# Talking-heads attention and a gated layer on one core: the first evictions, the second batch's scores and the order around the maximum

## The chip, the core and the metric

The kernel runs on one core of a Trainium2 chip. The core has TensorE (PE) for matrix products, VectorE (DVE), ScalarE (ACT) and GpSimd (POOL) for work on elements, and SyncE (SP), whose queue issues nearly all DMA transfers here. Each engine works through its own instructions in order; semaphores tie them together. The metric is the device time of one execution in microseconds (us).

## The reference

Attention with two mixings of the heads, and then a feed-forward layer with a gate. Cut to what matters:

```python
# q, k, v: (4, 12, 448, 64); w_pre, w_post: (12, 12)
scores = scale * np.matmul(q, k.transpose(0, 1, 3, 2))
scores = np.einsum('bhij,hg->bgij', scores, w_pre)
scores = scores - np.max(scores, axis=-1, keepdims=True)
attn = np.exp(scores)
attn = attn / (np.sum(attn, axis=-1, keepdims=True) + 1e-09)
attn = np.einsum('bhij,hg->bgij', attn, w_post)
x = np.matmul(attn, v)               # then to (4*448, 768)
h = x @ w_in                         # w_in: (768, 2048), float64 in memory
g = h * (1.0 / (1.0 + np.exp(-1.702 * h)))
out = g @ w_out                      # w_out: (2048, 768), float64 in memory
```

## The kernel before

**Steps.** The unit of the attention is a group of 10 query rows times 12 heads, which fills 120 partitions. A batch has 45 such groups, so there are 180 steps, and one loop over the step number `i` writes the whole program down. Of step `i` it issues, in this order: the gather of group `i + 4` out of a scratch tensor in DRAM (`gather`, SP's queue), the product that mixes the heads of group `i + 1` (`mix`, two instructions on PE), the second mixing of group `i - 2` (`post_whole`, PE, batch 0), the copies of its result for group `i - 3` (`keep_whole`, batch 0), the weights of the second mixing of group `i - 1` (`weigh_mix`, POOL), the maximum of group `i` (`peak`, L286, DVE), its exponential with the sum (`expo`, L293, ACT; the sum gets its small term on POOL, L299), then the jobs that are due (`run_jobs`), pieces of the feed-forward layer, score products, products with v, and last the reciprocal (`inverse`, L304, DVE). The next step's maximum stands behind that reciprocal on DVE.

**Scores.** They are made ahead, for a chunk of up to 120 query rows and one pair of heads at a time: `scores` (PE) into two banks of PSUM, `keep_scores` (copies to a tile `sc`, of which there are three), `send_scores` (SP's queue, to the scratch tensor `sd`). Batch 0 multiplies q and k in float32 (L233). Batches 1 to 3 split each operand into an upper and a lower float16 part and add three products (L243). For that, k and q of a batch are loaded once for a sum of squares (`squares`, ACT, six instructions of half a third each), a product with ones that adds it over the partitions (`join`, PE, then DVE), and small instructions on DVE for the scale (`scale`); and loaded again to be split (`upper_part` on ACT or POOL, `lower_part`, L201, on DVE). Batch 1's pairs are due in steps 34 to 73.

**Copies of mixed weights.** In batch 0, `post_whole` leaves 48 columns of blocks in one bank `pp` of PSUM; `keep_whole` copies it in two halves, the first on ACT (L385), the second on DVE (L382) or on ACT, by a count of what each engine has been given. Both stand ahead of the step's maximum and exponential. The two engines read one bank, so the second copy waits for the first.

**Jobs and tokens.** Each step gives every engine a budget of 4.3 (estimated us), kept up to 4.5. A job has a first step, what it must follow, an engine and an estimated cost; it is issued when its engine has half its cost left, or at once where it is marked urgent. The conversions of w_in and w_out are such jobs: 16 pieces, one due every five steps from step -6 on, each of three fetched parts (three buffers `w64`), five DVE instructions a part that turn float64 into float32 (L495 to L515), squares on ACT, a scale, an upper part and a lower part (L548, DVE), and a store.

**Start.** q and k of batch 0 come in thirds on SP's queue; then DVE builds the matrices of both mixings (`mixing`, `mixing_pair`, the latter with `wall`), and the first chunk's six pairs are made, evicted (one head on ACT, one on DVE), and sent, with the jobs of steps -6 to -1 between them. The first gathers stand behind the last send.

The order on every engine is thus fixed when the program is written; nothing is chosen on the chip.

Of the kernel before, what the change touches and what calls it, by code (L numbers as in the profile page):

```python
# [38 lines left out]
def attention_then_feed_forward(ctx, tc, q, k, v, w_pre, w_post, w_in, w_out, out):  # L39
# [81 lines left out]

    def load_whole(name, i):

        t = st[name, 0, i] = flow.tile(SH[name], F32, name=f"{name}f{i}_0", tag=f"{name}p{i}")
        w = t.shape[1]
        nc.sync.dma_start(out=t, in_=SRC[name][0][:, i * w:(i + 1) * w])

# [35 lines left out]
    def mixing(b):  # L163
        wa = keep.tile([KG, KG], F32, name=f"wa_{b}", tag="wa", bufs=2)
        if b == 0:
            nc.vector.tensor_scalar_mul(wa, w_mix.rearrange("p i g -> p (i g)"), 0.125)
            st["wa", b] = wa
            return
# [54 lines left out]
    def scores(b, c, pr, tag=("gen", 3)):  # L223
# [4 lines left out]
        w = NPAIR // THIRDS  # L228
        if b == 0:
            qf, kf = st["q", 0, pr // w], st["k", 0, pr // w]  # L230
            for x in range(2):
                rs = slice(x * D, (x + 1) * D)
                nc.tensor.matmul(  # L233
                    two[x][:n, :S], qf[rs, pr % w, i0:i0 + n], kf[rs, pr % w, :],
                    start=True, stop=True,
                )
            return two, done
# [131 lines left out]

    def keep_whole(i):  # L370
        b, g = steps[i]
        n = rows_of(g)[1]
        c, off = g // GPC, (g % GPC) * GI
        pp = row.pop(("pp", i))
        w = NR // 2
        for x in range(2):
            if off == 0:
                st["p", b, c, x] = mixed.tile([CP, w, H, CI], F32, name=f"pf{x}_{b}_{c}", tag=f"p{x + 1}")
            o = st["p", b, c, x].rearrange("p r h i -> p (r h) i")[:, :, off:off + n]
            src = pp[:, x * w * H:(x + 1) * w * H, :]  # L380
            if x and tokens["D"] > tokens["A"]:
                nc.vector.tensor_copy(o, src)  # L382
# [360 lines left out]
    for b in range(1, B):  # L743
        z = GPB * b
        sizes = {}
        for name, first, ready in (("k", z - 25, z - 17), ("q", z - 23, z - 17), ("v", z - 8, z + LAG + 7)):
            sq = []
            for i in range(THIRDS):
                a = staged(first, [], name, b, i, "a")
                sq.append(job(0, {"A": 1.6}, 0, lambda eng, name=name, i=i, b=b: squares(name, b, i, eng, 2),  # L750
                              after=[(a, SENT)], urgent=True))
# [3 lines left out]
            for i in range(THIRDS):  # L755
# [4 lines left out]
                a["stage"][1].extend([up, lo])  # L760
        job(0, "D", 0.4, lambda b=b: mixing(b), after=[sizes["k"], sizes["q"]], urgent=True)

# [61 lines left out]
    for i in range(THIRDS):  # L824
        for name in "kq":
            load_whole(name, i)
    for i, w in enumerate((w_pre, w_post)):
        nc.scalar.dma_start(out=wrep[:, i, :], in_=w.unsqueeze(0).to_broadcast([GI, H, H]))
    nc.scalar.dma_start(out=wall, in_=w_post.unsqueeze(0).to_broadcast([128, H, H]))
    nc.vector.memset(ones, 1.0)  # L830
    last_pp.append(ps.tile([128, 512], F32, name="sums", tag="av", bufs=1))
    nc.vector.memset(tops, 0.0)
    nc.scalar.activation(warm, tops[:, 0:1], AF.Exp)
# [14 lines left out]
    )  # L848
    mixing(0)
    def mixing_pair():  # L850
# [21 lines left out]

    mixing_pair()
    tags = [("gen", 3), ("mx", 2), ("pp", 2)]
    for pr in range(NPAIR):
        two, done = scores(0, 0, pr, tags[pr % 3])
        for x in done:
            x["done"] = True
        t = keep_scores(0, 0, pr, two, "AD")
        refill(2.0)  # L880
        run_jobs(pr - NPAIR)
        send_scores(0, 0, pr, t)
    for i in range(AHEAD):
        gather(i)
    for i in range(THIRDS):
        load_whole("v", i)
    sq = [job(1, {"A": 1.6}, 0, lambda eng, i=i: squares("v", 0, i, eng, 2), urgent=True) for i in range(THIRDS)]
    j = job(1, "D", 0.2, lambda: join("v", 0), after=sq, urgent=True)
# [52 lines left out]
    while quanta or i < N + LAG + 12:  # L941
# [12 lines left out]
        if 0 <= i - 3 < GPB:  # L954
            keep_whole(i - 3)
        if GPB <= i - LAG - 1 < N:
# [12 lines left out]
        if i < N:  # L969
            peak(i)  # L970
            spend("D", 0.62)
            expo(i)
            spend("A", 0.82)
        run_jobs(i)
        slot()
# [83 lines left out]
```

## Time and profile before

| | us |
|---|---|
| median of 3 runs | 1081.61 (1077.75 to 1081.65) |
| the profiled execution, in all | 1085.16 |
| its span, from the first instruction to the last | 1083.4 |
| PE busy | 934.9 |
| DVE busy | 656.2 |
| ACT busy | 595.4 |
| POOL busy | 383.5 |
| mean clock of PE, as a share of full speed | 0.935 |

The profile is one execution. An engine's busy time says how full it was on the whole; where a stage has its limit is read from the stretches and from what each engine waited for. A wait is put down to whatever came last by the profile. In the timeline an instruction of the second kind, "SPq", is an issue of a DMA by SP's queue. A count such as x3 stands for instructions merged in one row.

### The profile page before, as it was taken

How to read it: one execution, taken by the hardware profiler on the slowest of the kernel's cores; microseconds unless marked ns; L12 is line 12 of the kernel's file. 1: busy time of each engine (PE TensorE's matmuls, PEld its weight loads, DVE VectorE, ACT ScalarE, POOL GpSimd, SP SyncE). 2: the span in 40 equal slices, each digit the busy share in tenths (PEclk: the TensorE clock that was granted, in tenths of full speed). 3: DMA queues.
4: the chain of work that ended last, by engine and by line, in shares of the span. 5: the costliest groups of instructions: out<-in, count | busy, mean ns of one | idle time of the engine just before them, and what ended most of it. 6: DMA issues, size and time to landing. Idle time of an engine off the chain costs nothing.

```text
span 1083.4 us, 20018 instructions
## 1 busy us (share of the span) xinstructions
PE 934.9 (86%) x7344; PEld 549.3 (51%) x7344; DVE 656.2 (61%) x1444; ACT 595.4 (55%) x1389; POOL 383.5 (35%) x567
## 2 busy tenths in 40 slices
PE   3576766686779788889989899999899999999998
PEld 1244544463445454455546455556555666555554
DVE  4477856779878779655554457455654566433334
ACT  2455564656756766655655766665656555323332
POOL 0122212225534246443443255334534444200221
PEclk7689978988699998999999899999999999999999
DMA  7778777776757754755557456745564432234332
GB/s 247 229 270 313 258 259 229 246 243 213 246 162 247 226 196 145 248 168 154 150 186 224 148 174 193 224 141 162 181 205 142 142 107 82 88 114 142 117 117 80
DMA packets 67430, 200.95 MB, mean 185 GB/s; under 512 B 7764, under 2 KB 32468, under 8 KB 67332
## 3 DMA queue, kind: packets, MB, share of 16 engines
q1 hardware_dynamic: 66928, 199.59, 57.5%
q8 instruction: 58, 0.95, 0.4%
q14 instruction: 40, 0.33, 0.1%
q10 hardware_dynamic: 404, 0.09, 0.1%
HBM read 143.02 MB, written 56.62 MB: 184 GB/s over the span
## 4 chain that ended last, share of the span: by engine, by line
PE 59%; DVE 21%; ACT 8%; DMA 7%; issue 4%; SPq 0%; POOL 0%; ACTq 0%; DVEq 0%; POOLq 0%
PE po L637 18%; PE h L598 17%; PE mx L279 8%; PE av L420 4%; PE qk L243 3%; DVE nm L286 3%; DVE w_p L548 2%; PE pp L356 2%; DMA r<-sd 2%; DMA sd<-sc 2%; PE pp L358 2%; PE pp L357 2%; ACT waste L96 2%; DVE w_f L509 2%; DVE w_f L515 2%
## 5 line engine op out<-in xcount | busy, mean ns | idle before, releaser
L637 PE MATMUL po<-g,wt 128*128 128x448 f16 x1152 | 248.2, 359 | 10.7 <-DVE th L619 6.2
L598 PE MATMUL h<-x,wt 128*128 128x448 f16 x1152 | 244.1, 355 | 4.4 <-ACT sc L253 2.5
L279 PE MATMUL mx<-r,wa 120*120 120x448 f32 x360 | 187.7, 605 | 60.6 <-ACT e L293 38.6
L343 POOL TENSOR_TENSOR a<-w,a 120x448 f16<-120x448 f32 x135 | 150.8, 1117 | 124.3 <-issue 69.4
L637 PEld LDWEIGHTS <-wt 128*128 128x128 f16 x1152 | 110.5, 99 | 133.3 <-issue 49.6
L329 POOL TENSOR_SCALAR w<-e,rs 120x448 f32<-120x448 f32 x135 | 91.0, 674 | 239.6 <-DVE rs L304 220.4
L598 PEld LDWEIGHTS <-wt 128*128 128x128 f16 x1152 | 109.2, 99 | 115.6 <-issue 29.7
L293 ACT ACTIVATE e<-mx,nm 120x448 f32<-120x448 f32 x180 | 113.3, 629 | 84.2 <-DVE nm L286 51.1
L337 ACT ACTIVATE a<-e,rs 120x448 f16<-120x448 f32 x135 | 91.0, 674 | 118.7 <-DVE rs L304 118.7
L667 DVE SCALAR_TENSOR_TENSOR acc<-po,ct,acc 128x448 f32<-128x448 f32 x141 | 96.0, 682 | 83.8 <-PE po L637 81.8
L616 ACT ACTIVATE th<-h,ct 128x448 f32<-128x448 f32 x64 | 40.5, 633 | 150.4 <-PE h L598 136.1
L619 DVE SCALAR_TENSOR_TENSOR th<-th,h 128x448 f32<-128x448 f32 x64 | 39.6, 619 | 137.3 <-ACT th L616 137.3
L286 DVE TENSOR_REDUCE nm<-mx 120x1 f32<-120x448 f32 x180 | 109.1, 606 | 13.7 <-PE mx L279 13.7
L279 PEld LDWEIGHTS mx<-r,wa 120*120 120x120 f32 x360 | 61.9, 194 | 101.9 <-ACT e L293 55.0
L356 PE MATMUL pp<-wp,a 120*112 120x120 f16 x540 | 97.3, 222 | 18.8 <-DVE p L393 18.2
L253 ACT COPY sc<-qk 120x448 f32<-120x448 f32 (+1 forms) x186 | 89.5, 531 | 35.5 <-PE qk L243 15.3
L299 POOL TENSOR_SCALAR rs<-sm 120x1 f32<-120x1 f32 x180 | 56.5, 314 | 134.2 <-ACT e L293 122.2
L358 PE MATMUL pp<-wp,a 120*112 120x120 f16 x540 | 96.7, 221 | 0.0
L357 PE MATMUL pp<-wp,a 120*112 120x120 f16 x540 | 96.5, 220 | 0.0
L393 DVE TENSOR_TENSOR p<-pp,p 112x480 f16<-112x480 f32 x135 | 87.1, 646 | 3.0 <-ACT p L390 2.9
L356 PEld LDWEIGHTS <-a 120*112 120x112 f16 x540 | 72.5, 134 | 27.4 <-DVE p L393 13.3
L357 PEld LDWEIGHTS <-a 120*112 120x112 f16 x540 | 72.8, 135 | 19.8 <-issue 13.6
(126 smaller groups left out, 1305.8 us busy)
## 6 DMA issues: line engine op xcount, KB each, us to landing
wt<-wd SPq DMA_DIRECT2D x64, 768.0 KB, 5.3
r<-sd SPq DMA_DIRECT2D x176, 210.0 KB, 4.5
sd<-sc SPq DMA_DIRECT2D x72, 420.0 KB, 6.1
w<-in_moe_w_in_dram SPq DMA_DIRECT2D x24, 512.0 KB, 6.6
w<-in_moe_w_out_dram SPq DMA_DIRECT2D x24, 512.0 KB, 5.3
wd<-w_p SPq DMA_DIRECT2D x16, 768.0 KB, 3.6
sd<-sc SPq DMA_DIRECT2D x24, 308.0 KB
out_dram<-acc SPq DMA_DIRECT2D x24, 224.0 KB, 1.9
```

Of the source, the lines that this page charges most:

```text
L279: nc.tensor.matmul(mx[:K, :S], st["wa", b][:K, :K], row.pop(("r", i))[:K, :], start=True, stop=True)
L286: nc.vector.tensor_reduce(nm[:K], row["mx", i][:K, :S], axis=AX.X, op=ALU.max, negate=True)
L293: nc.scalar.activation(e[:K], row.pop(("mx", i))[:K, :S], AF.Exp, bias=row.pop(("nm", i))[:K, 0:1], scale=1.0, accum_out=sm[:K, 0:1],)
L329: nc.gpsimd.tensor_scalar(w[:K], e[:K], row["rs", i][:K, 0:1], 1.0, op0=ALU.mult, op1=ALU.mult)
L337: nc.scalar.activation(a1[:K], row.pop(("e", i))[:K], AF.Copy, scale=row.pop(("rs", i))[:K, 0:1])
L343: nc.gpsimd.tensor_tensor(a2[:K], row.pop(("w", i))[:K], row["a1", i][:K], op=ALU.subtract)
L356: nc.tensor.matmul(o, a1[:K, js], wp1[:K, :, :n], start=True, stop=False)
L357: nc.tensor.matmul(o, a1[:K, js], wp2[:K, :, :n], start=False, stop=False)
L358: nc.tensor.matmul(o, a2[:K, js], wp1[:K, :, :n], start=False, stop=True)
L598: nc.tensor.matmul(h, w[:, i, c, fc * 128:(fc + 1) * 128], x[:, j, c, :], start=(n == 0), stop=(n == len(terms) - 1),)
L637: nc.tensor.matmul(po, w[:, j, fc, e * 128:(e + 1) * 128], g[:, i, fc, :], start=(n == 0), stop=(n == len(terms) - 1),)
L667: nc.vector.scalar_tensor_tensor(a, po, c, a, op0=ALU.mult, op1=ALU.add)
```

## The change

Six things change. (1) At the start the jobs of step -6 (the fetch of w_in's first piece) come first, then all six pairs of the first chunk are made, evicted and sent, and only then the matrices of the mixings are built and the jobs of steps -6 to -1 run. (2) PE gets 10 products of a tile of ones ahead of the first scores and 16 behind the last, whose results nobody reads. (3) Batch 1's scores use float32 operands, as batch 0's do; its k and q are loaded once, third by third in steps 22, 26 and 30, and the squares, joins, scales and parts of batch 1's k and q fall away. (4) The second half of the copies of mixed weights is always DVE's, and stands behind the step's maximum and exponential. (5) v's squares of batch 0 stand in steps 1, 3 and 5 instead of all in step 1. (6) The squares of a later third come one step later each.

```diff
-    def load_whole(name, i):
-        t = st[name, 0, i] = flow.tile(SH[name], F32, name=f"{name}f{i}_0", tag=f"{name}p{i}")
+    def load_whole(name, b, i):
+        t = st[name, b, i] = flow.tile(SH[name], F32, name=f"{name}f{i}_{b}", tag=f"{name}p{i}")
...
-        if b == 0:
-            qf, kf = st["q", 0, pr // w], st["k", 0, pr // w]
+        if b < 2:
+            qf, kf = st["q", b, pr // w], st["k", b, pr // w]
...
-    def keep_whole(i):
+    def keep_whole(i, halves):
...
-        for x in range(2):
+        for x in halves:
...
-            if x and tokens["D"] > tokens["A"]:
+            if x:
                 nc.vector.tensor_copy(o, src)
...
+        if b == 1:
+            for i in range(THIRDS):
+                for name in "kq":
+                    job(z - 23 + 4 * i, None, 0, lambda name=name, i=i: load_whole(name, 1, i), urgent=True)
         for name, first, ready in (("k", z - 25, z - 17), ("q", z - 23, z - 17), ("v", z - 8, z + LAG + 7)):
+            if b == 1 and name != "v":
+                continue
...
-                sq.append(job(0, {"A": 1.6}, 0, lambda eng, name=name, i=i, b=b: squares(name, b, i, eng, 2),
+                sq.append(job(first + SENT + i, {"A": 1.6}, 0, lambda eng, name=name, i=i, b=b: squares(name, b, i, eng, 2),
                               after=[(a, SENT)], urgent=True))
...
+    def idle_products(n):
+        for _ in range(n):
+            nc.tensor.matmul(last_pp[0][:, :128], ones, ones, start=True, stop=True)
+
+    idle_products(10)
...
-    mixing(0)
...
-    mixing_pair()
     tags = [("gen", 3), ("mx", 2), ("pp", 2)]
+    run_jobs(-NPAIR)
     for pr in range(NPAIR):
         two, done = scores(0, 0, pr, tags[pr % 3])
         for x in done:
             x["done"] = True
-        t = keep_scores(0, 0, pr, two, "AD")
+        send_scores(0, 0, pr, keep_scores(0, 0, pr, two, "AD"))
+    mixing(0)
+    mixing_pair()
+    for x in range(-NPAIR, 0):
         refill(2.0)
-        run_jobs(pr - NPAIR)
-        send_scores(0, 0, pr, t)
+        run_jobs(x)
+    idle_products(16)
...
-    sq = [job(1, {"A": 1.6}, 0, lambda eng, i=i: squares("v", 0, i, eng, 2), urgent=True) for i in range(THIRDS)]
+    sq = [job(1 + 2 * i, {"A": 1.6}, 0, lambda eng, i=i: squares("v", 0, i, eng, 2), urgent=True) for i in range(THIRDS)]
...
         if 0 <= i - 3 < GPB:
-            keep_whole(i - 3)
+            keep_whole(i - 3, (0,))
...
             expo(i)
             spend("A", 0.82)
+        if 0 <= i - 3 < GPB:
+            keep_whole(i - 3, (1,))
         run_jobs(i)
```

What this does to the order on the engines is shown at three places. The first is SP's queue at the start, before: `sc_0_4` and `sc_0_5` are the evicted scores of the last two pairs, `w_0_64` the buffers of a conversion's three parts, `r` a gathered group.

```order
L258 DMA sd_0_90<-sc_0_4_218 120x896
L488 DMA w_0_64_0_235<-in_moe_w_out_dram 128x1024
L488 DMA w_0_64_1_238<-in_moe_w_out_dram 128x1024
L488 DMA w_0_64_2_240<-in_moe_w_out_dram 128x1024
L258 DMA sd_0_90<-sc_0_5_230 120x896
L269 DMA r_243<-sd_0_90 120x448
```

SP's queue at the same place, after:

```order
L258 DMA sd_0_90<-sc_0_4_198 120x896
L258 DMA sd_0_90<-sc_0_5_206 120x896
L488 DMA w_0_64_0_246<-in_moe_w_out_dram 128x1024
L488 DMA w_0_64_1_249<-in_moe_w_out_dram 128x1024
L488 DMA w_0_64_2_251<-in_moe_w_out_dram 128x1024
L269 DMA r_269<-sd_0_90 120x448
```

The three fetches of w_out stood ahead of the last send and now stand between it and the first gather.

The second place is DVE at the start, before: the end of `mixing_pair` (`wp`), the first three eviction copies (`sc`), and the first instruction of the conversion of w_in (`w_0_f`).

```order
L868 TENSOR_SCALAR wp_84<-wp,s_wp 120x120
L869 SCALAR_TENSOR_TENSOR wp_85<-wp,s_wp,wp_84 120x120
L253 COPY sc_0_0_161<-qk_0_0_1_158 120x448
L253 COPY sc_0_1_176<-qk_0_1_1_173 120x448
L253 COPY sc_0_2_184<-qk_0_2_1_181 120x448
L495 TENSOR_SCALAR w_0_f_187<-w_0_64_0_164 128x512
```

DVE after, from the last eviction copy to the conversion's first instruction:

```order
L253 COPY sc_0_5_206<-qk_0_5_1_203 120x448
L166 TENSOR_SCALAR wa_210<-w_mix 120x120
L863 TENSOR_REDUCE rows_w<-wall 128x12
L866 TENSOR_REDUCE tops<-rows_w 128x1
L867 TENSOR_SCALAR tops<-tops 128x1
L868 TENSOR_SCALAR e_wp<-tops 128x1
L872 RECIPROCAL s_wp<-e_wp 128x1
L873 TENSOR_SCALAR s_wp<-s_wp 128x1
L874 TENSOR_TENSOR wp<-wrep,sel 120x120
L880 TENSOR_SCALAR wp_84<-wp,s_wp 120x120
L881 SCALAR_TENSOR_TENSOR wp_85<-wp,s_wp,wp_84 120x120
L495 TENSOR_SCALAR w_0_f_222<-w_0_64_0_155 128x512
```

All six evictions now stand ahead of the set-up, and the conversion stands behind both, where it had run between the later evictions.

The third place is DVE around the maximum in steps 8 and 9, before: `nm` is the maximum, `rs` the reciprocal, `pf` the copy's second half out of the bank `pp`, `w_0_n` a join's sum.

```order
L304 RECIPROCAL rs_442<-rs_442 120x1
L382 COPY pf_0_0_383<-pp_428 112x24x10
L286 TENSOR_REDUCE nm_475<-mx_426 120x1
L109 TENSOR_REDUCE w_0_n<-pp_466 128x1
L81 TENSOR_SCALAR w_0_n<-w_0_n 128x1
```

DVE after, in the same step of the program:

```order
L304 RECIPROCAL rs_451<-rs_451 120x1
L286 TENSOR_REDUCE nm_484<-mx_436 120x1
L382 COPY pf_0_0_408<-pp_438 112x24x10
L109 TENSOR_REDUCE w_0_n<-pp_476 128x1
L81 TENSOR_SCALAR w_0_n<-w_0_n 128x1
```

The copy stood between the reciprocal and the next maximum, and now stands behind the maximum.

## Rows read from the trace of the kernel before

**Rows 1.** Busy time by stretch: PE, PEld, DVE, ACT, POOL; clock, DMA share, GB/s.

```profile
40.00:240.00 200.00, 144.88 (x859) 93.65 (x859) 145.28 (x373) 117.56 (x326) 50.14 (x111) 0.86 0.77 258
240.00:480.00 240.00, 197.21 (x1605) 115.87 (x1604) 190.14 (x391) 154.56 (x360) 110.73 (x144) 0.91 0.65 206
480.00:1083.40 603.40, 579.72 (x4856) 334.57 (x4853) 306.70 (x647) 316.58 (x691) 221.88 (x305) 0.99 0.48 149
```

**Rows 2.** Timeline of the start: start us, length us, engine, line, operation, [idle before].

```profile
6.72 5.87 SPq L488 DMA_DIRECT2D w<-in_moe_w_in_dram  x3
...
12.27 0.40 DVE L851 TENSOR_REDUCE rows_w<-wall 128x12 f32<-128x144 f32 x1 [5.29 <-DMA wall<-in_w_post_dram]
...
14.44 1.68 DVE L253 COPY sc<-qk 120x448 f32<-120x448 f32 x3
...
18.14 0.69 DVE L515 SCALAR_TENSOR_TENSOR w_f<-w,w_f 128x512 int32<-128x512 int32 x1
...
19.15 0.53 ACT L253 COPY sc<-qk 120x448 f32<-120x448 f32 x1 [7.75 <-DMA sd<-sc]
...
34.37 1.70 SPq L269 DMA_DIRECT2D r<-sd  x4
...
37.39 3.31 PE L279 MATMUL mx<-r,wa 120*120 120x448 f32 x4 [18.42 <-DMA r<-sd]
```

**Rows 3.** Busy time by stretch of 2 us, columns as in the first group.

```profile
6.00:8.00 2.00, 2.00 (x8) 0.79 (x6) 0.51 (x2) 0.53 (x1) 0.00 (x0) 1.00 0.93 330
...
36.00:38.00 2.00, 0.61 (x1) 0.47 (x2) 0.00 (x0) 0.00 (x0) 0.00 (x0) 0.50 0.88 251
```

**Rows 4.** Copies of mixed weights by line: durations ns min/median/max; who waited for them.

```profile
L385 ACT COPY pf<-pp x58: 338/371/394, 52.3 to 247.0; 112x240 f32<-112x240 f32 x56, 112x192 f32<-112x192 f32 x2
...
  DVE pf L382: 33.2, 17
...
L382 DVE COPY pf<-pp x32: 381/407/409, 52.7 to 243.8; 112x240 f32<-112x240 f32 x32
```

**Rows 5.** Timeline of one step of batch 0, DVE and ACT.

```profile
81.88 0.41 DVE L382 COPY pf<-pp 112x240 f32<-112x240 f32 x1 [2.04 <-ACT pf L385]
...
82.21 0.61 DVE L286 TENSOR_REDUCE nm<-mx 120x1 f32<-120x448 f32 x1
...
82.92 0.63 ACT L293 ACTIVATE e<-mx,nm 120x448 f32<-120x448 f32 x1 [1.07 <-DVE w_n L109]
```

**Rows 6.** Timeline: copies on DVE behind blocks of squares; squares of k by line.

```profile
138.44 0.41 DVE L382 COPY pf<-pp 112x240 f32<-112x240 f32 x1 [3.03 <-ACT pf L385]
...
148.65 0.41 DVE L382 COPY pf<-pp 112x240 f32<-112x240 f32 x1 [4.48 <-ACT pf L385]
...
217.19 0.41 DVE L382 COPY pf<-pp 112x240 f32<-112x240 f32 x1 [5.05 <-ACT pf L385]
...
L96 ACT ACTIVATE waste<-ka x18: 565/577/583, 132.5 to 601.8; 128x448 bf16<-128x448 f32 x18
```

**Rows 7.** Timeline: lower parts on DVE; one pair's score products on PE.

```profile
190.89 3.27 DVE L201 SCALAR_TENSOR_TENSOR qp<-qb,s_q,qp 128x896 f16<-128x896 f32 x3
...
195.81 0.78 PE L243 MATMUL qk<-kp,qp 64*120 64x448 f16 x6
...
85.46 1.02 PE L233 MATMUL qk<-kf,qf 64*120 64x448 f32 x4
...
49.59 1.85 PE L233 MATMUL qk<-kf,qf 64*120 64x448 f32 x4
```

**Rows 8.** Timeline of PE: joins of squares of later batches.

```profile
372.02 0.39 PE L108 MATMUL pp<-mq,ones 128*128 128x6 f32 x2 [2.71 <-ACT p L390]
...
464.56 0.39 PE L108 MATMUL pp<-mv,ones 112*128 112x6 f32 x2 [3.23 <-ACT p L390]
...
604.50 0.39 PE L108 MATMUL pp<-mk,ones 128*128 128x6 f32 x2 [2.79 <-ACT p L390]
```

More of the change, by code (lines that the diff above doesn't have):

```diff
@@ L120, in load @@
         nc.sync.dma_start(out=t, in_=SRC[name][b][:, i * w:(i + 1) * w])
-    def load_whole(name, i):
-        t = st[name, 0, i] = flow.tile(SH[name], F32, name=f"{name}f{i}_0", tag=f"{name}p{i}")
+    def load_whole(name, b, i):
+        t = st[name, b, i] = flow.tile(SH[name], F32, name=f"{name}f{i}_{b}", tag=f"{name}p{i}")
         w = t.shape[1]
-        nc.sync.dma_start(out=t, in_=SRC[name][0][:, i * w:(i + 1) * w])
+        nc.sync.dma_start(out=t, in_=SRC[name][b][:, i * w:(i + 1) * w])
     def squares(name, b, i, eng, n=1):
@@ L166, in mixing @@
             nc.vector.tensor_scalar_mul(wa, w_mix.rearrange("p i g -> p (i g)"), 0.125)
-            st["wa", b] = wa
+            st["wa", 0] = st["wa", 1] = wa
             return
@@ L373, in keep_whole @@
         c, off = g // GPC, (g % GPC) * GI
-        pp = row.pop(("pp", i))
+        pp = row["pp", i]
         w = NR // 2
-        for x in range(2):
+        for x in halves:
             if off == 0:
@@ L760, in attention_then_feed_forward @@
                 a["stage"][1].extend([up, lo])
-        job(0, "D", 0.4, lambda b=b: mixing(b), after=[sizes["k"], sizes["q"]], urgent=True)
+        if b > 1:
+            job(0, "D", 0.4, lambda b=b: mixing(b), after=[sizes["k"], sizes["q"]], urgent=True)
     conv_done = {}
@@ L825, in attention_then_feed_forward @@
         for name in "kq":
-            load_whole(name, i)
+            load_whole(name, 0, i)
     for i, w in enumerate((w_pre, w_post)):
@@ L885, in attention_then_feed_forward @@
     for i in range(THIRDS):
-        load_whole("v", i)
-    sq = [job(1, {"A": 1.6}, 0, lambda eng, i=i: squares("v", 0, i, eng, 2), urgent=True) for i in range(THIRDS)]
+        load_whole("v", 0, i)
+    sq = [job(1 + 2 * i, {"A": 1.6}, 0, lambda eng, i=i: squares("v", 0, i, eng, 2), urgent=True) for i in range(THIRDS)]
     j = job(1, "D", 0.2, lambda: join("v", 0), after=sq, urgent=True)
```

## Prediction

> **What bounds the kernel now.** I read the busy time by stretch first [rows 1]. From 480 us on, PE is busy for 579.72 of 603.4 us at a clock of 0.99: that stretch is PE's, and only its 23.7 us of gaps can be won. From 40 to 240 us (batch 0's 45 steps of mixing) no engine is full: DVE 145.28 of 200, PE 144.88 at 0.86 of its clock, ACT 117.56. There a step is a ring: maximum on DVE, exponential on ACT, reciprocal on DVE, next maximum. What holds the ring up is whatever stands in it on either engine. From 240 to 480 us PE (197.21 of 240) and DVE (190.14) are both nearly full. Ahead of 40 us little computes: PE waits 18.42 us for the first gathered rows [rows 2]. A microsecond won ahead of 480 moves everything behind it, since PE's later order is fixed and is the same in both kernels.
>
> Next the waits of the copies of mixed weights [rows 4]: the second half of the copy, L382 on DVE, waited 33.2 us in 17 cases for the first half, L385 on ACT. One such case in detail [rows 5]: DVE stands idle for 2.04 us until ACT's copy is over, copies its own half (0.41), then takes the maximum (0.61); ACT, which had nothing else left, waits 1.07 us for that and only then begins the exponential.
>
> **The change, part by part**, against the profiled execution's own time (1085.16 us, its span 1083.4). The median of the runs shown is 1081.61, 3.55 lower, so the same sum is taken off the median.
>
> *Start.* Today DVE waits for `wall` (12.27) and sets up the post weights before its first eviction copies (14.44), so the first send waits too [rows 2]. After the change all six evictions stand ahead. But the third fetch of w_in holds SP's queue until 6.72 + 5.87 = 12.59, and sends stand behind it in both kernels. So send 0 leaves at best 2.5 us earlier; its data queue behind w_in's on the DMA engines. Pair 3's eviction, which waits for send 0, comes at 19.15 today; I take 18.0 (bounds 16.6 and 19.2), and 1.6 us for each next pair (0.43 MB at the 258 GB/s of [rows 1]), so DVE's last eviction ends near 18.0 + 3.2 + 0.6 = 21.8. Today DVE converts w_in in those waits; now the set-up follows the evictions (12.27 to 14.44, about 2.2 us, and 0.2 for `mixing`), and three parts of 2.7 us each (the first one today: from 14.44 + 1.68 = 16.12 to 18.14 + 0.69 = 18.83 [rows 2]) begin at 24.2 and end at 32.3. SP's order matters here: the three fetches of w_out now stand behind the last send and ahead of the first gather, and each waits until DVE has released its buffer. So the first gather is issued near 33 instead of 34.37, and has half a megabyte ahead of it that it had not. Today the first mix follows its issue by 3.0 us (37.39); with that half megabyte 3 to 5, so 36 to 38. The gain is 0 (bounds -2 and +3).
>
> The idle products cost PE time that it has. The first ten stand ahead of scores that run at a clock of 1.00 anyway [rows 3]. The other sixteen wait for nothing and follow the last scores, so they end some 10 us ahead of the first mix, whose four instructions took 3.31 us at a clock of 0.50 [rows 2, 3]. I take 0; at twice the clock those four would take half, so 1.6 us is the upper bound. The Trainium skill (TensorE: Matmul & The Clock Gate, "What's actually happening") has the half rate as the default and activity as what lifts it; by it, too, products that end long before the mix do nothing for it, and by it products set against the mix would be worth that 1.6.
>
> *Second halves of the copies.* Of 45 steps, 32 had the second half on DVE; 13 go over from ACT (58 copies = 45 + 13) [rows 4]. They had been on ACT where DVE was loaded: 13 x 0.41 = 5.3 us more for DVE, of which I count half, 2.7, since the planner then moves conversions to lighter steps. Behind the maximum, the wait for ACT's half remains, but no longer holds up the exponential: ACT goes on 1.07 us earlier. DVE's own release moves by less: it ends at ACT's copy + 0.41 instead of + 0.96, that is 0.55 earlier. Of the 17 cases five fall in stretches that other parts of this change clear, and one in the tail; 11 remain, at 0.8 between 0.55 and 1.07: 8.8. Net +6 (bounds 11 x 0.55 - 5.3 = +1 and 11 x 1.07 = +12). Waiting behind the half are now the conversions, which have room, and the reciprocal, which needs the exponential anyway.
> The Trainium skill (PSUM — Partial Sum Buffer, "PSUM bank collisions raise a hardware error") forbids two engines in one bank and quadrant at a time, reads against reads included, so the wait for ACT's half is no choice of this kernel. The 33.2 us agree. By it none of the wait goes away, only its place; were the wait itself removed, up to 33.2 us would be at stake.
>
> *Batch 1's scores in float32.* Gone for batch 1: 12 squares on ACT, two joins and scales, six upper and six lower parts, six loads with their issues on SP. The squares stood in blocks of six: DVE waited 3.03 and 4.48 us at their ends [rows 6], with six squares of 0.58 us (and a read of each sum) between ACT's exponential and its copy. Without them ACT's chain is some 4.2 us shorter in each step, but DVE's own work then fills the step: I take 6.5 of the 7.5 us (bounds 5 and 8). The six lower parts take 2 x 3.27 = 6.5 us of DVE, in line ahead of the next maximum [rows 7]; the gap they leave is partly filled by conversions, which come earlier: I take 5 (2 to 8). The added price is on PE: a pair of heads takes 1.02 us in float32 against 0.78 as three float16 terms; at half clock 1.85 [rows 7]. 24 pairs x 0.24 = 5.8 us; the first 12 run where PE has gaps, so I take -3 (bounds 0 and -9). The whole loads reuse the buffers of batch 0's operands, two steps after their last scores, so SP doesn't stall on them.
>
> *Squares spread.* v of batch 0: four of six squares leave step 1. DVE is full there with conversions, so +0.5 (0 to 2.3 = 4 x 0.58). v of batch 1: DVE waited 5.05 us behind six squares [rows 6]; two now stay, two go to each of the next two steps: +2 (0 to 3). Batches 2 and 3: PE stood idle for 2.71, 3.23 and 2.79 us at joins that wait for ACT [rows 8]. A join now comes behind fewer squares in its own step; with the steps around them I take +5 (0 to 12). The q loads of these batches are let go one by one, which costs nothing, as their parts come 9 steps later.
>
> **Sum:** 0 + 6 + 6.5 + 5 - 3 + 0.5 + 2 + 5 = 22. 1085.2 - 22 = 1063.2 for the profiled execution, 1081.6 - 22 = 1059.6 for the median: **1060 us**.
>
> **Rivals.** *DVE is the bound.* If DVE's work alone sets batch 0 and what follows to 300 us, waits that vanish only uncover its next instruction. Then the gain is DVE's net work: 6.5 for the lower parts and about 2.5 for joins and scales, less 5.3 for the copies: 3.7, and **1078 us**. For it: 145 of 200 us busy and 190 of 240. Against it: the 33.2 us of its own waiting, all behind ACT.
> *PE becomes the bound (slower).* From step 34 on, when batch 1's scores start, the new products run at 1.2 GHz (a clock of 0.5 in the rows) in stretches with few gaps. A pair then costs 1.85 - 0.78 = 1.07 more, 24 pairs 25.7 us, and gains on ACT and DVE behind step 34 are worth nothing: left are the first squares (6.5), three quarters of the copies (4.5) and 1 for the rest. 12 - 25.7 = -14: **1095 us**. It decides when a pair costs over 12 / 24 = 0.5 more than now. For it: PE at 0.86 of its clock, and rows at 1.85. Against it: PE had 55 us of gaps in that stretch, and at full clock a pair costs 0.24.
> *The ring closes fully.* Each case gives back 1.07 and DVE absorbs the 13 copies (+12), the squares give 8 + 3, the parts 8, the spread 8, float32 costs 2: 37 us, **1045 us**. For it: ACT was idle for the 1.07 in each such step. Against it: steps in which DVE is full don't move at all.
> *The change doesn't do what it says.* At the start this is my forecast already: idle products and earlier evictions end in the same first mix.
>
> **How the numbers follow.** Forecast 0.67, the ring closing fully 0.15, DVE the bound 0.11, PE the bound 0.07. The forecast's own terms have half-widths of 2.5, 5.5, 1.5, 3, 4.5, 1, 1.5 and 6 us; taken as independent (root of the sum of squares) they spread some 10 us, 1050 to 1070. The range reaches to 1041 to take in most of the 1045 case and to 1077, short of most of the 1078 case: 1041 to 1077. A measurement here tells 0.5%, 5.4 us, from no change, so faster means under 1076.2: nearly all of the forecast, all of the 1045 case and a third of the 1078 case less what the forecast loses there: 0.82. Same: 0.11. Slower: 0.07.
>
> **What would show it.** Right: the first mix between 36 and 38 us; no DVE wait ahead of a maximum for a copy on ACT, and exponentials that start right behind ACT's copy in 11 or more steps; batch 0's last step some 15 to 20 us earlier than today; a pair of batch 1 near 1.02 us on PE; the stretch that PE fills unchanged in length but for a few us. Wrong: the first mix under 34 us (then SP's order didn't matter); DVE over 90% busy from 40 to 220 us; a PE clock lower than 0.86 there with pairs at 1.85.

## The result and the profile after

The changed kernel takes 1049.47 us in the median of 6 runs (1046.81 to 1050.65), the kernel before 1082.45 (6 runs beside it). The ratio is 0.9701, with a 95% interval of 0.968 to 0.9723: 33 us less, where 22 were forecast. It lies inside the range of 1041 to 1077.

The page of the changed kernel's profile, busy time and PE's clock in 40 slices:

```profile
span 1048.0 us, 19948 instructions
PE 923.6 (88%) x7344; PEld 544.6 (52%) x7344; DVE 650.7 (62%) x1434; ACT 580.4 (55%) x1353; POOL 389.2 (37%) x563
PEclk9789888988899999999999999999999999999999
```

Busy time by stretch, columns as in [rows 1]. The first two are cut at the same places of the program as there, within some 2 us (first maximum, first of batch 1, step 88). The last two go from the maximum of step 88 to the end, for the changed kernel and then for the kernel before:

```profile
38.00:221.00 183.00, 137.58 (x809) 87.60 (x808) 148.23 (x372) 100.64 (x284) 56.24 (x107) 0.88 0.81 267
221.30:458.50 237.20, 200.33 (x1615) 114.88 (x1614) 182.33 (x379) 158.22 (x368) 112.07 (x145) 0.95 0.65 209
458.50:1048.00 589.50, 570.32 (x4846) 330.93 (x4843) 306.13 (x652) 314.68 (x687) 219.85 (x304) 1.00 0.48 153
482.26:1083.40 601.14, 577.46 (x4846) 333.46 (x4843) 304.94 (x645) 315.75 (x688) 221.88 (x305) 0.99 0.48 150
```

Batch 0's 45 steps take 183 us instead of 200, with DVE now busy for 148.23 of them (81%, before 73%) though its own work grew by 3 us only. ACT's fell by 17. The last stretch is shorter by 12 us, and two things make that up: PE does 4846 products in both, now in 570 instead of 577 us, with its clock at 1.00 and no longer 0.99 (a hundredth of 601 us is 6), and its gaps fall from 23.7 to 19.2.

Where the 35.4 us between the two spans arise is seen best from one landmark per step, the start of its maximum on DVE. Read from the timelines of all kernels below, this is how much later (+) or earlier (-) than in the changed kernel it comes, in us, up to the last step, 179:

```
step          0      6     21     33     45     60     74     92    110    116    132    179
before     +0.8   +5.0   +6.0  +13.8  +18.6  +13.2  +11.7  +23.8  +26.2  +32.4  +33.7  +35.3
```

So the start gave 0.8, steps 0 to 6 4.2, batch 0 as a whole 18; then 7 were lost again by step 74, and 24 won behind it, half of them from step 92 on, where PE is the bound. All runs below are looked at with this landmark. Where a kernel's program differs from the changed one only at one place, the drift elsewhere shows what is chance: some of them come out 2 us ahead between steps 10 and 21, where nothing of theirs differs, so a drift of 2 us means nothing. Up to about step 85 a single entry can also be off by some 4 us, since a maximum stands behind more or less of the jobs on DVE: one of the kernels below falls 7.1 us behind at step 41 and wins 2.8 of them back at step 42.

### The profile page after: what moved, and what is told of

Its sections match the earlier page's. It is cut to its first block, busy times and chain, and to the rows that moved or that the text cites. A ratio compares the mean times of both kernels' runs of the same rounds, so it can differ in the third digit from the quotient of the medians.

```text
span 1048.0 us, 19948 instructions
## 1 busy us (share of the span) xinstructions
PE 923.6 (88%) x7344; PEld 544.6 (52%) x7344; DVE 650.7 (62%) x1434; ACT 580.4 (55%) x1353; POOL 389.2 (37%) x563
## 4 chain that ended last, share of the span: by engine, by line
PE 64%; DVE 23%; ACT 6%; issue 4%; DMA 2%; POOL 1%; ACTq 0%; SPq 0%; DVEq 0%; POOLq 0%
PE po L637 19%; PE h L598 17%; PE mx L279 9%; PE av L420 4%; DVE w_p L548 3%; DVE w_f L509 3%; PE qk L243 2%; PE pp L356 2%; DVE nm L286 2%; PE pp L319 2%; PE pp L358 2%; PE pp L357 2%; DVE w_f L515 2%; DVE w_f L499 2%; PE qk L233 2%
## 5 line engine op out<-in xcount | busy, mean ns | idle before, releaser
L637 PE MATMUL po<-g,wt 128*128 128x448 f16 x1152 | 241.7, 353 | 11.1 <-DVE th L619 6.2
L279 PE MATMUL mx<-r,wa 120*120 120x448 f32 x360 | 184.4, 596 | 60.9 <-ACT e L293 42.6
L637 PEld LDWEIGHTS <-wt 128*128 128x128 f16 x1152 | 108.8, 98 | 127.2 <-issue 41.4
L598 PEld LDWEIGHTS <-wt 128*128 128x128 f16 x1152 | 108.7, 98 | 114.1 <-issue 28.1
L356 PE MATMUL pp<-wp,a 120*112 120x120 f16 x540 | 96.3, 220 | 15.2 <-DVE p L393 14.8
L299 POOL TENSOR_SCALAR rs<-sm 120x1 f32<-120x1 f32 x180 | 64.1, 356 | 109.4 <-ACT e L293 97.5
L358 PE MATMUL pp<-wp,a 120*112 120x120 f16 x540 | 95.7, 219 | 0.0
L357 PE MATMUL pp<-wp,a 120*112 120x120 f16 x540 | 95.5, 219 | 0.0
```

What stands on the lines that cost most here:

```text
L279: nc.tensor.matmul(mx[:K, :S], st["wa", b][:K, :K], row.pop(("r", i))[:K, :], start=True, stop=True)
L356: nc.tensor.matmul(o, a1[:K, js], wp1[:K, :, :n], start=True, stop=False)
L357: nc.tensor.matmul(o, a1[:K, js], wp2[:K, :, :n], start=False, stop=False)
L358: nc.tensor.matmul(o, a2[:K, js], wp1[:K, :, :n], start=False, stop=True)
L598: nc.tensor.matmul(h, w[:, i, c, fc * 128:(fc + 1) * 128], x[:, j, c, :], start=(n == 0), stop=(n == len(terms) - 1),)
L637: nc.tensor.matmul(po, w[:, j, fc, e * 128:(e + 1) * 128], g[:, i, fc, :], start=(n == 0), stop=(n == len(terms) - 1),)
```

## Experiments: the parts undone one at a time

All of these are the changed kernel with one part undone; ratios are to the kernel before, run beside them. The changed kernel's own is 0.9701. Added up, undoing the parts costs 6.4, 11.7, 3.0 and 16.9 us and, for the start, -1.9: 36 us against the 33 of the whole, so the parts add up as well as their intervals (3 to 4 us each way) can tell.

**The order around the maximum.** First the whole part undone:

```diff
-            if x:
+            if x and tokens["D"] > tokens["A"]:
...
-            keep_whole(i - 3, (0,))
+            keep_whole(i - 3, (0, 1))
...
-        if 0 <= i - 3 < GPB:
-            keep_whole(i - 3, (1,))
```

> The changed kernel with its fourth part undone: the second half of the copies of mixed weights again ahead of the step's maximum, on DVE or ACT by the count of tokens. The forecast's theory: this part is worth 6 us, so 1055 to 1056, and the waits of 1.06 to 1.07 us of ACT ahead of the exponential come back in 11 or more steps. Rival, from the starts of the maxima side by side: between steps 6 and 21 the kernels drift apart by 1 us only, because DVE is full in the steps between, so this part alone is worth 0 to 2 us: 1049 to 1052.

Measured: 1055.87 us, ratio 0.976 (0.9729 to 0.9791): 0.0059 of 1081, 6.4 us. Then the same with only the place undone, all 45 second halves on DVE but ahead of the maximum (the last two hunks alone):

> The changed kernel with the second half of the copies on DVE in all 45 steps, but ahead of the maximum as in the kernel before. It parts the place from the engine. If the place is what counts (forecast: 8.8 us for it, -2.7 for the 13 copies that go to DVE), this is slower than with the part undone altogether: 1058 to 1059. If the engine counts (ACT relieved of 13 copies), it is as fast as the changed kernel: 1050.

Measured: 1060.84 us, 0.9803 (0.9758 to 0.9847), 11 us slower than the changed kernel. So by the times the place behind the maximum is worth 11 us, and giving DVE the other copies costs 4.6 of them; but the intervals of these two runs overlap, so the 4.6 alone is not told from nothing. (With the part undone, DVE makes 30 of the 45 second halves, so 15 go over, not 13: 0.3 us each.) By the landmark the two kernels end 9.8 and 5.0 us behind. Of the 9.8 only 6.4 arise up to step 74. The other 3.4 come at steps 79 and 104, where both kernels have the same instructions in the same order; there PE's clock falls in one of them and not in the other, as the last section shows. The place itself is thus shown to be worth 6 us, and 11 with what follows it in these runs. One step of the changed kernel, DVE and ACT, shows what the place does (columns as in [rows 5]):

```profile
54.07 0.60 DVE L286 TENSOR_REDUCE nm<-mx 120x1 f32<-120x448 f32 x1
...
54.68 0.37 ACT L385 COPY pf<-pp 112x240 f32<-112x240 f32 x1
...
54.93 0.66 ACT L293 ACTIVATE e<-mx,nm 120x448 f32<-120x448 f32 x1
55.08 0.41 DVE L382 COPY pf<-pp 112x240 f32<-112x240 f32 x1 [0.41 <-ACT pf L385]
```

The maximum is over before ACT comes to its copy, so the exponential follows the copy with no idle time, where it had waited 1.07 us in [rows 5]. In the kernel before 20 exponentials of steps 0 to 51 stand behind an idle time of 1.04 to 1.19 us that DVE ended; in the changed kernel none, with the part undone 20 again, with the place alone undone 22. Of the exponentials of steps 1 to 51, 21 have no idle time ahead of them in the changed kernel (8 in the kernel before), 11 of these right behind ACT's copy (before none). In all, the idle time ahead of them fell from 69.7 to 53.3 us; it is 64.0 with the part undone and 70.4 with the place alone undone.

What is left is still a wait for the maximum: each exponential of batch 0 that waits starts at most 0.12 us behind the maximum's end. In the step shown here the maximum stands behind a conversion on DVE. The profile puts most of these waits down to POOL, because an instruction there ends a moment later than the maximum (89.78 against 89.77 us in this step):

```profile
89.17 0.60 DVE L286 TENSOR_REDUCE nm<-mx 120x1 f32<-120x448 f32 x1
89.41 0.37 POOL L309 TENSOR_SCALAR wr<-wp,rs 120x120 f32<-120x120 f32 x1 [0.78 <-DVE rs L304]
...
89.86 0.63 ACT L293 ACTIVATE e<-mx,nm 120x448 f32<-120x448 f32 x1 [2.16 <-POOL wr L309]
```

DVE's own wait for ACT's half didn't go, as the Trainium skill's rule on one bank for one engine had it (PSUM — Partial Sum Buffer, "PSUM bank collisions raise a hardware error"); by line, the second halves of the changed kernel and who kept DVE waiting ahead of them:

```profile
L382 DVE COPY pf<-pp x45: 346/398/409, 51.0 to 233.7; 112x240 f32<-112x240 f32 x44, 112x192 f32<-112x192 f32 x1
...
  ACT pf L385: 21.0, 14
```

That is 21.0 us against 33.2 [rows 4], and the maximum no longer stands behind it.

**Batch 1's scores** as three float16 products again, with all their preparation:

```diff
-        if b < 2:
+        if b < 1:
             qf, kf = st["q", b, pr // w], st["k", b, pr // w]
...
-            if b == 1 and name != "v":
-                continue
...
```

> The changed kernel with its third part undone: batch 1's scores again as three float16 products, with squares, joins, scales and parts of its k and q, the squares one third per step. The forecast's theory: the preparation is worth 11.5 us and the float32 products cost 3, so 1058. Rival A: the preparation was hidden once its squares are spread, so only 2 to 4 us: 1052. Rival B: the float32 products cost PE the full 5.8 us of 24 pairs and more behind step 45, where the gain of the changed kernel shrinks from 18.6 to 13 us: then undoing gives back 5 us there and loses about 13 ahead of it, again 1057 to 1058, but with batch 0 over 13 us longer and batch 1's steps 45 to 75 about 5 us shorter than in the changed kernel.

Measured: 1061.31 us, 0.9809 (0.9774 to 0.9843): 11.7 us, some 3 us more than any of the three, and nearest to the forecast's theory. The drift has both halves of it: the undone kernel falls 10 us behind between steps 21 and 45, wins 4.6 back up to step 74, and loses them again by step 92, where its conversions, put off by the parts, are still to be done (its last one stands in step 80, the changed kernel's in step 75). The 4.6 are little more than what single entries can be off by, and no run has the float32 products without the loss of the preparation, so the two prices are not parted here.

```
step          0      6     21     33     45     60     74     92    110    116    132    179
b1_f16     +0.2   +0.2   -2.3   +5.8   +7.8   +6.7   +3.2   +8.3   +8.7   +8.7   +8.7   +8.7
```

**The squares.** Batch 0's v in one block, and then all later batches in blocks:

```diff
-    sq = [job(1 + 2 * i, {"A": 1.6}, 0, lambda eng, i=i: squares("v", 0, i, eng, 2), urgent=True) for i in range(THIRDS)]
+    sq = [job(1, {"A": 1.6}, 0, lambda eng, i=i: squares("v", 0, i, eng, 2), urgent=True) for i in range(THIRDS)]
```

> The changed kernel with its fifth part undone: the six squares of batch 0's v all in step 1. The forecast's theory: DVE is full there, so 0.5 us: 1050. Rival, from the starts of the maxima: steps 2 to 5 are 4.3 us ahead of the kernel before, and nothing else of the change touches them, so 4 us: 1053 to 1054.

Measured: 1052.49 us, 0.9729 (0.9691 to 0.9767): 3 us, by the landmark 2. The intervals overlap, so it is not told from nothing by the times alone; the landmark puts it into steps 2 to 6. With the six squares in one block the exponential of step 2 starts at 49.41 us, in the changed kernel at 47.18.

```diff
-                sq.append(job(first + SENT + i, {"A": 1.6}, 0, lambda eng, name=name, i=i, b=b: squares(name, b, i, eng, 2),
+                sq.append(job(0, {"A": 1.6}, 0, lambda eng, name=name, i=i, b=b: squares(name, b, i, eng, 2),
```

> The changed kernel with its sixth part undone: squares of a batch again as soon as their loads are two steps old, six in a block. The forecast's theory: 2 us for v of batch 1 and 5 for batches 2 and 3, so 1056 to 1057. Rival A, from the starts of the maxima: 6 us at step 40 and up to 12 us behind step 100, so 1063 to 1067. Rival B: the gains behind step 100 come from elsewhere (conversions that end earlier, a clock of 1.00 for 0.99), so 1051 to 1053.

Measured: 1066.36 us, 0.9857 (0.9828 to 0.9887): 16.9 us, the largest part of all, and rival A.

```
step           0      6     21     33     45     60     74     92    110    116    132    179
late_block  +0.2   +0.2   -2.4   -2.6   -0.2   -0.3   +3.8   +8.8   +8.8  +15.2  +16.5  +18.0
```

2.4 us arise at batch 1's v (step 40), 4.1 at batch 2's k and q, 5.0 at its v, 6.4 at batch 3's k and q, 2.8 behind that. The 5.0 are a join that waits 3.23 us for ACT, and a clock of 0.66 in the 5 us behind it, which is 1.7 us of work lost: 4.9. The 6.4 can be read nearly in full. PE's timeline with the squares in blocks, at batch 3's k and q:

```profile
587.10 0.59 PE L108 MATMUL pp<-mk,ones 128*128 128x6 f32 x2 [2.79 <-ACT p L390]
...
597.75 2.40 PE L637 MATMUL po<-g,wt 128*128 128x448 f16 x6 [2.47 <-ACT sc L253]
```

And PE's busy time and clock around these two gaps, by 2 us (columns as in [rows 1]):

```profile
584.00:586.00 2.00, 0.31 (x1) 0.00 (x0) 1.44 (x4) 1.94 (x7) 0.64 (x1) 1.00 0.81 246
586.00:588.00 2.00, 0.90 (x4) 0.68 (x5) 0.28 (x2) 2.00 (x5) 0.26 (x1) 0.78 0.86 307
588.00:590.00 2.00, 2.00 (x9) 0.95 (x8) 1.32 (x5) 0.22 (x2) 1.61 (x3) 0.50 0.93 203
590.00:592.00 2.00, 2.00 (x19) 1.53 (x18) 0.53 (x5) 1.04 (x3) 0.00 (x0) 0.86 0.93 325
...
596.00:598.00 2.00, 0.25 (x1) 0.10 (x1) 0.69 (x2) 1.97 (x6) 0.00 (x0) 0.84 0.03 10
598.00:600.00 2.00, 2.00 (x7) 0.97 (x6) 0.00 (x1) 1.14 (x3) 0.00 (x0) 0.50 0.39 86
600.00:602.00 2.00, 2.00 (x9) 1.03 (x8) 1.82 (x5) 0.47 (x1) 0.41 (x1) 0.80 0.18 72
```

ACT is full (1.94 to 2.00 of 2 us) with squares ahead of the copies that PE waits for; PE stands idle, and then its clock falls from 1.00 to 0.50, 2.4 to 1.2 GHz, so that the work behind the gap runs at half speed until the clock is back. From the clock column, what is lacking to 1.00 times 2 us: 0.44 + 1.00 + 0.28 behind the first gap and 0.32 + 1.00 + 0.40 behind the second, 3.4 us besides the gaps of 5.3. Some 0.2 of the 0.32 fell into the gap itself (PE was busy for 0.25 of those 2 us), so 3.2 us of work were lost. The changed kernel at the same place, PE's timeline and its stretches, has one gap and no fall:

```profile
584.02 1.30 PE L637 MATMUL po<-g,wt 128*128 128x448 f16 x6 [2.36 <-ACT sc L253]
```

```profile
582.00:584.00 2.00, 0.00 (x0) 0.00 (x0) 0.41 (x1) 1.97 (x7) 0.00 (x0) 1.00 0.89 325
584.00:586.00 2.00, 1.98 (x10) 1.13 (x10) 0.92 (x4) 1.41 (x3) 0.00 (x0) 1.00 0.94 306
586.00:588.00 2.00, 2.00 (x22) 1.39 (x21) 2.00 (x7) 1.29 (x4) 1.13 (x2) 1.00 0.69 239
```

5.3 + 3.2 - 2.4 = 6.1, against 6.4 by the landmark. So the spread took away the join's wait of 2.79 us and both falls of the clock, and left the second gap nearly as it was: in the changed kernel four squares still stand in a row ahead of those copies, the last two of k and the first two of q. The Trainium skill (TensorE: Matmul & The Clock Gate, "What's actually happening") has it that activity holds the clock up and idleness gives it back to half; the trace agrees in that both falls come with a gap, but the changed kernel's gap of 2.36 us brings none. At this place half of what the spread is worth is the clock. Of the 2.8 us further on, 1.5 are a fall of the clock at step 149, behind a gap of 2.42 us that the changed kernel has too, without a fall; the programs are the same there, so this is not the squares' own price.

**The spread alone**, put on the kernel before (the same two lines there), to see whether the parts' worth adds up:

> The kernel before with the fifth and sixth parts of the change alone: squares spread over steps, in all batches, batch 1's k and q among them. If the parts' worth adds up (3 us for v of batch 0 and 17 for the rest, found by undoing them, and up to 5 more for batch 1's k and q, which the changed kernel doesn't have): 1056 to 1061. Rival: what the spread is worth rests on the other parts, above all on conversions that end earlier: 1068 or more.

Measured: 1064.33 us, 0.9823 (0.9789 to 0.9857), between the two expectations: 19.2 us, about the 20 (3 + 17) that undoing them had cost, and nothing of the 5 more for batch 1's k and q. By the landmark 4.3 of its 22.0 us arise up to step 74 and 17.7 behind it. So the worth behind step 74 stands by itself; the parts ahead of it add up less well.

**The start.** The first two parts undone, the old order with no idle products:

```diff
-    idle_products(10)
...
+    mixing(0)
+    mixing_pair()
-    run_jobs(-NPAIR)
     for pr in range(NPAIR):
...
-        send_scores(0, 0, pr, keep_scores(0, 0, pr, two, "AD"))
-    mixing(0)
-    mixing_pair()
-    for x in range(-NPAIR, 0):
+        t = keep_scores(0, 0, pr, two, "AD")
         refill(2.0)
-        run_jobs(x)
-    idle_products(16)
+        run_jobs(pr - NPAIR)
+        send_scores(0, 0, pr, t)
```

> The changed kernel with its first two parts undone: set-up ahead of the evictions, conversions of w_in between them, w_out's fetches ahead of the last send, no idle products. The forecast's theory: nothing, because the first gather is held up either way, so 1049 to 1051 and the first maximum within 1 us of 38.5. Rival: the idle products raise the clock for the first steps, and the start is worth 3 us or more: 1053.

Measured: 1048.54 us, 0.9684 (0.9647 to 0.972): no difference. The changed kernel without the two calls of `idle_products`:

> The changed kernel without its 26 idle products. The forecast's theory: nothing (0 to 1.6 us), 1049 to 1051, and the first four instructions of the mix at 3.31 us as with them. Rival: the first scores run slower without them and delay the sends: the first maximum 1 us or more later.

Measured: 1048.29 us, 0.9682 (0.9646 to 0.9719): none either. Part of the rival is true all the same: PE's first scores, two pairs in the changed kernel and then four without idle products, do run slower without them:

```profile
6.89 1.77 PE L233 MATMUL qk<-kf,qf 64*120 64x448 f32 x8 [1.14 <-DMA qf<-in_q_dram]
```

```profile
5.83 5.90 PE L233 MATMUL qk<-kf,qf 64*120 64x448 f32 x16 [5.83 <-DMA qf<-in_q_dram]
```

That is 0.9 us a pair against 1.5. It is worth nothing because the sends stand behind w_in's fetches on SP's queue: the last of these fetches is out at 11.65 us in the changed kernel and at 12.54 without idle products, the first send leaves at 11.78 and at 12.66, and the first maximum comes 0.2 us earlier without them. Then the one order that the forecast holds to blame, turned round:

```diff
-    for x in range(-NPAIR, 0):
+    for x in range(-NPAIR, -1):
         refill(2.0)
         run_jobs(x)
     idle_products(16)
     for i in range(AHEAD):
         gather(i)
+    refill(2.0)
+    run_jobs(-1)
```

> The changed kernel with the job of step -1, the three fetches of w_out's first piece, issued behind the first four gathers instead of ahead of them. If SP's order is what ate the gain of the earlier evictions, the gathers leave as soon as the last send has landed, near 25 us instead of 32.07, and the first mix runs near 28; the first maximum then waits for DVE's conversions of w_in, which end at 31.5, so it comes near 31.6 instead of 38.5: 7 us, 1042 to 1043. Rival: the DMA engines are what is full, the gathers land late all the same, or the conversion of w_out comes later by as much: 1047 to 1050.

Measured: 1042.31 us, 0.9626 (0.959 to 0.9663): 8.1 us less than the changed kernel by the ratios, 7.0 at the first maximum and 7.9 at the last by the landmark. The start of the changed kernel, timeline:

```profile
26.12 5.75 SPq L488 DMA_DIRECT2D w<-in_moe_w_out_dram  x3
...
32.07 1.70 SPq L269 DMA_DIRECT2D r<-sd  x4
...
36.63 3.31 PE L279 MATMUL mx<-r,wa 120*120 120x448 f32 x4 [18.29 <-DMA r<-sd]
...
38.48 0.62 DVE L286 TENSOR_REDUCE nm<-mx 120x1 f32<-120x448 f32 x1 [6.96 <-PE mx L279]
```

And with the gathers first:

```profile
24.80 1.68 SPq L269 DMA_DIRECT2D r<-sd  x4
...
26.52 5.40 SPq L488 DMA_DIRECT2D w<-in_moe_w_out_dram  x3
27.48 3.31 PE L279 MATMUL mx<-r,wa 120*120 120x448 f32 x4 [8.49 <-DVE w_f L503]
...
31.48 0.62 DVE L286 TENSOR_REDUCE nm<-mx 120x1 f32<-120x448 f32 x1
```

(The profile puts the mix's wait down to L503, which ended just before; the mix reads only gathered rows and its own matrix.) The last send had landed by 24.8. SP's queue, standing at fetches that waited for DVE to release their buffers, had held the gathers back for 7.3 us. The first maximum now waits for the conversions on DVE, no longer for the gathers.

## Experiments: the price of float32 and the fastest kernel

Batch 2's scores in float32 too, to price the products where PE is the bound:

```diff
-        if b < 2:
+        if b < 3:
             qf, kf = st["q", b, pr // w], st["k", b, pr // w]
...
-            if b == 1 and name != "v":
+            if b < 3 and name != "v":
```

> The changed kernel with batch 2's scores in float32 too. Its pairs are due in steps 79 to 118, and PE is full from step 85 on. It measures the price of the float32 products where PE is the bound. The forecast's theory: 24 pairs x 0.24 = 5.8 us, less 1 to 3 us for joins and stalls of the preparation that go: 1052 to 1054. Rival: the preparation is what costs, as in batch 1 (12 us by undoing that part), so 1038 to 1043. Second rival: in PE's stretch the preparation's gaps and the products cancel: 1048 to 1051.

Measured: 1045.49 us, 0.9648 (0.9608 to 0.9688): 5.7 us less by the ratios, but the intervals touch; 4.8 by the landmark, of which 1.9 is the chance drift ahead of step 21.

```
step          0      6     21     33     45     60     74     92    110    116    132    179
b2_f32     +0.2   +0.2   -1.9   -1.8   -1.8   -1.7   -3.6   -7.5   -5.6   -5.2   -4.8   -4.8
```

The drift has the two prices apart: 5.8 us won between steps 60 and 92, where the preparation is gone, and 2.7 lost from 92 to 132, where PE is full and multiplies in float32. None of the three expectations holds: not a loss of 3 to 5, not 6 to 11 won, and 1045.5 is under the 1048 to 1051 of prices that cancel.

> The changed kernel with the first gathers ahead of w_out's fetches and batch 2's scores in float32. If the two add up: the run with the gathers ahead (1042.3) plus or minus what float32 for batch 2 does by itself, so 1045 to 1047 by the forecast's theory and 1031 to 1036 by the rival.

Measured, both together: 1043.32 us, 0.9621 (0.9586 to 0.9657). It lies between the two expectations, and the two don't add up to anything that can be told from the gathers alone. In the profiled execution 3.4 us went to the clock: PE has gaps of 2.08 and 2.13 us there, with a clock of 0.79 in the 8 us around each; with batch 2 alone in float32 the same gaps are 1.94 and 2.13 us, with a clock of 1.00.

> The changed kernel with the first gathers ahead of w_out's fetches and without idle products: the candidate for the fastest. If idle products are worth nothing here either, 1041 to 1043, and the first mix's four instructions take 3.31 us as with them. Rival: nearer to the mix (8.5 us instead of 18 between the last of them and the mix) they hold the clock, and without them the time is 1044 or more.

Measured, gathers first and no idle products: 1041.71 us, 0.9636 (0.9614 to 0.9658), inside the first expectation, with the first mix at 3.31 us. Idle products are worth nothing here either. The fastest kernels are those with the gathers first, 1042 us, 3.7% under the kernel before and some 7 us under the changed one.

## Why the prediction was right, and where its sum was not

*Start (0 forecast).* Right, and by its own steps: third fetch of w_in over at 7.33 + 4.32, set-up and three conversions behind the evictions, first gather at 32.07 (forecast near 33), first mix at 36.63 (36 to 38). With the gathers first, 7 us came that SP's order had kept. Idle products: 0, as forecast, but one reason for it was wrong, and the number came out by luck there. The prediction took the first scores to run at a clock of 1.00 anyway, from the row of 6 to 8 us in [rows 3]; but that 1.00 doesn't fit their times. Without idle products they take 1.5 us a pair, with them 0.9, and SP's queue kept that from counting. The first mix takes 3.31 us with them and without. By the Trainium skill's rule on the clock (TensorE: Matmul & The Clock Gate, "What's actually happening"), as the prediction reads it, products that end long before the mix do nothing for it; the trace agrees, and gave none of the 1.6 us.

*Second halves (+6).* Right in sum (6.4) and in kind. The two terms are known less well: the place is 11 by the times and 6.4 by the landmark up to step 74, for 8.8; the copies -4.6 by the times and -1.4 by the landmark, for -2.7. Whether the planner took half of the copies' price away is not shown. The exponentials right behind ACT's copy, 11 of them, are the number that the forecast gave as its sign.

*Batch 1's scores (6.5 + 5 - 3 = 8.5).* 11.7 by the times, 8.7 by the landmark. The float32 term of -3 is near the 4.6 that undoing it gave back up to step 74, though that drift is good to some 4 us only. The preparation was then sized a little low, since the conversions that it puts off come later, behind step 74; that this is the reason is argued, not shown. Of batch 1's 24 pairs in the changed kernel 19 take 0.99 to 1.03 us on PE, and two 1.85; PE's timeline of one of each:

```profile
186.72 1.02 PE L233 MATMUL qk<-kf,qf 64*120 64x448 f32 x4
...
314.58 1.85 PE L233 MATMUL qk<-kf,qf 64*120 64x448 f32 x4
```

So PE didn't become the bound at 1.2 GHz, and that rival falls: in batch 0's steps its clock rose from 0.86 to 0.88, behind them from 0.91 to 0.95. (The 55 us of gaps that the prediction holds against it are those of 40 to 240 us; from 240 to 480, where most of these pairs run, PE had 42.8.)

*Squares (0.5 + 2 + 5).* Here the sum failed. v of batch 0: 2 to 3 for 0.5. It is true that DVE is full there, but with four squares fewer the exponential of the next step starts 2.2 us sooner. v of batch 1: 2.4 by the landmark, for 2. Batches 2 and 3: 18 by the landmark, for 5. The step that failed read "PE stood idle for 2.71, 3.23 and 2.79 us at joins that wait for ACT". It counted 5 of these 8.7 us of waits [rows 8] as the price, and put the clock behind them at nothing. What the runs showed in its place: the waits went whole at two of the joins (3.23 and 2.79 us), and behind each of them the clock had fallen to a half, which costs 1.7 us more each time; a third fall, behind the copies of scores at batch 3's k and q, went too, though its gap stayed. The prediction read the clock of that stretch as 0.99 and took it for full; the missing hundredth of 603 us is 6 us. Not read in full are the 4.1 us at batch 2's k and q, and 1.3 of the 2.8 us behind batch 3's; 1.5 of these are the fall at step 149, which is not the squares' own.

*The rivals.* DVE as the bound (1078) was wrong although DVE is busier now (81%): its waits lay behind ACT, and going away they shortened the ring. The ring closing fully (1045) came nearer to the time than the forecast, but not by its own terms: the copies and the preparation gave about what the forecast has, the rest came from PE's stretch. That stretch was to be "unchanged in length but for a few us"; it lost 12.

## What to carry to other kernels

A block of work on an engine that is not the bound costs what stands behind it: six squares in a row on ACT, 0.70 us apart, stopped PE at a join for 2.79 us, and a fall of PE's clock behind the gap cost 1.7 us more; with two per step that wait was gone. Where two such jobs meet in one step, as the last of k and the first of q do, their squares stand in a row again. Of two copies that must follow each other, the one on the engine of the ring goes behind the ring's own step, even if it then waits as long. And an issue in a queue that waits for a buffer holds everything behind it, here the first gathers for 7.3 us: look what stands behind each such issue before the gain of an earlier send is counted.

## What the runs showed of the hardware

I had not expected gaps that differ so little to end so differently: behind 2.79 and 2.47 us of idle PE the granted clock fell from 1.00 to 0.50, and behind one of 2.36, at the same place of the program, it stayed at 1.00. The length of a gap alone doesn't decide it. The changed kernel and the run with the place alone undone have the same instructions in the same order on every engine from step 48 on; PE's timeline just ahead of the maximum of step 104, in the one and in the other:

```profile
529.11 2.43 PE L637 MATMUL po<-g,wt 128*128 128x448 f16 x12 [2.42 <-DVE th L619]
```

```profile
537.24 4.11 PE L637 MATMUL po<-g,wt 128*128 128x448 f16 x12 [2.42 <-DVE th L619]
```

The same twelve products behind the same gap take 2.43 us at a clock of 1.00 and 4.11 us where the clock has fallen (0.57 in the 4 us behind the gap): 1.7 us by a fall that the program doesn't explain. In the kernel before, a gap of 3.26 us at 357.65 is followed by a clock of 1.00, and one of 2.10 us at 614.79 by 0.50. What decides it was not tried. So one execution's drift holds falls of the clock that another execution of the same order may not have, and each is worth 1.7 us.

Nor had I expected that runs whose programs agree up to step 40 and further differ by 2 us between steps 10 and 21, and then keep that difference to the end. Most of it is the clock again: from the maximum of step 14 to that of step 17 the changed kernel takes 11.75 us at a clock of 0.85, and the run with the later squares in blocks, with the same program up to step 40, 10.11 us at 1.00.
